# The 64-row tail of a gradient product on TensorE: full-height matmuls with zero rows, or pairs of half-height matmuls in runs across two steps

## The chip, the core and the metric

The kernel runs on one core of a Trainium2 chip. The metric is the device time of one execution in microseconds (us); lower is better. The engines are named as the profile names them: PE (TensorE, matmuls), PEld (its weight loads), DVE (VectorE), ACT (ScalarE), POOL (GpSimd) and SP (SyncE, which here only issues DMAs). Each engine runs its own instructions in a fixed order that is set when the program is built; they wait for one another through semaphores.

## The reference

The kernel computes a forward pass and all its gradients: a layer norm, a long convolution whose kernel comes from a state space model, and a gated feed-forward block (SwiGLU) that gates the convolution's result.

```python
def _B_ref(x, w1, w3, w2):
    gate = jnp.einsum("bsd,df->bsf", x, w1)
    up = jnp.einsum("bsd,df->bsf", x, w3)
    h = _silu(gate) * up
    out = jnp.einsum("bsf,fd->bsd", h, w2)
    return out

x = A_u                                   # 1 x 2048 x 576, bf16
xn = _layernorm(x, axis=-1)
s = _A_ref(xn, ...)                       # the convolution, by FFT
g = _silu(_B_ref(xn, B_w1, B_w3, B_w2))   # w1, w3: 576 x 4608, w2: 4608 x 576
out = x + s * g
# and the gradients of out for grad_out with respect to all inputs but B_x
```

The product around which the change stands is the gradient with respect to `h`. With `go` the gradient at the output of the feed-forward block (2048 tokens x 576), it is `gh = go @ w2.T` (2048 x 4608). It is summed over the 576 model columns. 576 is four times 128 and a rest of 64.

## The kernel before, in words

**Stages.** The kernel makes the forward feed-forward gate beside the forward convolution (0 to about 500 us of the profiled execution), then the feed-forward output and `go` (to about 640 us), then a backward stage of 18 *groups*, each of 256 of the 4608 hidden columns (`phase6_group`, from about 625 to 1321 us), and last the input gradients (`phase6_inputs`, to the end).

**One group of the backward stage** has on PE: (1) the product `gh` in four *steps* of `make(s)` (line L1936); (2) two pieces of the gradient of `w2` (`phase6_grad2`, L1977), one placed behind step 1 and one behind step 3; (3) the gradients of `w1` and `w3` (`phase6_grad13`, L2005, and for the last 64 model rows L2014 and L2016), which need the results of DVE on `gh`. In groups 0 to about 10 the backward convolution is fed in between (its transforms on PE at L932, L942 and L952, and long products on DVE at L963 to L971 and L1453); in groups 11 to 17 it is the sums for the state space parameters (PE at L1537, DVE at L1542 and L1545).

**The product `gh`.** A step makes 4 tiles of 128 tokens, k = 0, 1 in each half j = 0, 1 of the sequence, 256 hidden columns wide. Two PSUM banks (`ph[0]`, `ph[1]`, 128 x 512 in fp32) hold j = 0 and j = 1, with k = 0 and 1 side by side. Each tile is the sum of five matmuls, four over 128 model rows and a fifth, the *tail*, over the last 64. The tail also runs at 128 rows: the transposed `go` of the rest (`goTt`) has its lower 64 partitions set to zero by a memset (in `ffn_output`), and the columns of the row buffers of `w2` behind column 576 (`w2rows`, `backward`) are set to zero by a memset before the DMA transposes make `w2T` of them. So a step has 20 matmuls, a group 80, the kernel 1440, 288 of them tails:

```python
for k in range(2):
    t = s * 2 + k
    for j in range(2):
        ...
        steps.append((self.goTt[:, tt * P:(tt + 1) * P], w2T[:, :, nfull, :]))
```

ACT then copies the two banks to `gh` in bf16 (L1939), and DVE multiplies `gh` into two tiles `gu_n` and `gg_n` (L1954), which `phase6_grad13` reads and which SP stores.

**PSUM.** The eight banks of the backward stage are three for the product (`ps_h`), two for the weight gradients (`ps_gw`, tiles `pgw`, taken in turn by all of `phase6_grad2` and `phase6_grad13`) and three for the convolution and the parameter sums. A tile of a pool takes the bank used longest ago, and its first matmul waits until ACT has copied what stood there.

**Transposes of `go`.** `turn_go` turns each of the 16 tiles of `go` by five PE transposes to a PSUM tile and two ACT copies, the second for the rest of 64 rows (L1310 to L1312).

**The loads of `w2`.** `w2row_load` issues two DMAs per group from SP (L1830), 128 rows of 576 columns each; two groups later a pair of DMA transposes (L1851) makes `w2T`.

**What sets the order.** Every piece of work carries a due time (`self.at`), and a scheduler fixes each engine's order when the program is built, by due times, by the readiness it computes, and by `issue_after`, which puts one instruction behind another on the same engine. `self.sc` and `self.sp` keep ACT's copies and SP's DMAs in the order of the code.

The forward gate has a product of the same kind: at L1132 the 64-row rest of `w1` and of `w3` stand on partitions 0 to 63 and 64 to 127 and are multiplied as two matmuls of 64 rows and 512 columns, `pg` and `pu`, behind one another in the order. In the backward stage L2014 and L2016 are two matmuls of 64 output columns each, `gg_n` and `gu_n`, in turn.

## Time and profile before

| | us |
|---|---|
| median of the three timed runs | 1637.4 |
| the three runs | 1630.57, 1641.31, 1637.4 |
| the profiled execution's own time | 1642.12 |
| span from its first to its last instruction | 1640.3 |

| engine | busy us | share |
|---|---|---|
| PE | 1565.6 | 95% |
| DVE | 1386.0 | 84% |
| ACT | 840.3 | 51% |
| POOL | 516.9 | 32% |

A group of instructions is written with its line, engine, operation and tiles (out<-in), and its count; busy time counts time that two of its instructions share once, so that 1440 matmuls that each last 274 ns from start to end take 169.7 us, since the next begins while the last is still draining. The *pitch* below is the time from the start of one matmul to the start of the next. Where a row of the timeline merges several instructions, its time runs from the first one's start to the last one's end. In such rows 128*128 or 64*128 is the part of the array that a matmul uses, rows by columns of the weights.

### The profile page before, as it was taken

The numbers are of one execution on the slowest core, as the hardware profiler recorded it, in microseconds if no ns is written. First come the engines' busy times: TensorE is split into PE (matmuls) and PEld (weight loads), VectorE is DVE, ScalarE is ACT, GpSimd is POOL, SyncE is SP. The second block draws the span as 40 slices with busy tenths as digits, with TensorE's granted clock in tenths as the row PEclk, the third lists the DMA queues.
The fourth block names the chain that finished last, engine by engine and source line by source line (L and its number), as shares of the span: only waits on it lengthen the run. The fifth ranks groups of instructions, "written<-read, shape, count | busy, mean of one in ns | idle before, by whom it ended". The sixth has DMA issues, their size and how long they took to land. (4 is left out here: it accounts for less than half of the span.)

```text
span 1640.3 us, 34408 instructions
## 1 busy us (share of the span) xinstructions
PE 1565.6 (95%) x13331; PEld 1146.1 (70%) x13331; DVE 1386.0 (84%) x2145; ACT 840.3 (51%) x1520; POOL 516.9 (32%) x862
## 2 busy tenths in 40 slices
PE   6899999999999998999999999999999999998997
PEld 2454444444457777888888888888888787886786
DVE  8889999799965655998988999699999944987897
ACT  6989998766652115556555665655555401010011
POOL 6746765532252110111111111112212341524232
PEclk9999999999999999999999999999999999999999
DMA  7999999998999997576695756799999999999993
GB/s 237 344 346 362 373 347 382 371 271 250 324 284 217 236 208 229 158 216 195 190 252 164 213 186 183 207 262 243 266 259 250 245 245 245 240 195 201 241 230 87
DMA packets 616156, 408.26 MB, mean 249 GB/s; under 512 B 424698, under 2 KB 558426, under 8 KB 611386
## 3 DMA queue, kind: packets, MB, share of 16 engines
q1 hardware_dynamic: 561232, 277.45, 68.0%
q0 software_dynamic: 36576, 116.69, 21.7%
q10 hardware_dynamic: 18186, 11.95, 2.5%
q8 instruction: 104, 1.70, 0.4%
q14 instruction: 58, 0.48, 0.1%
HBM read 128.52 MB, written 188.76 MB: 193 GB/s over the span
## 5 line engine op out<-in xcount | busy, mean ns | idle before, releaser
L2005 PEld LDWEIGHTS <-xn_bf 128*128 128x128 bf16 x2304 | 224.2, 98 | 26.8 <-issue 0.8
L2059 PEld LDWEIGHTS <-acts 128*128 128x128 bf16 x1974 | 192.0, 98 | 56.8 <-DMA acts<-GG_dram 4.7
L1989 POOL DMA_DIRECT2D out_dram<-gw x72 | 47.2, 656 | 527.3 <-ACT gw L1983 285.1
L1542 DVE TENSOR_TENSOR pr_q<-et_ps,pz 128x1024 f32<-128x1024 f32 x144 | 176.0, 1222 | 34.7 <-PE et_ps L1537 25.5
L1123 PEld LDWEIGHTS <-xnT 128*128 128x128 bf16 x1152 | 107.7, 98 | 128.6 <-issue 21.1
L1545 DVE TENSOR_REDUCE S_all<-pr_q 128x32 f32<-128x1024 f32 x144 | 175.3, 1217 | 3.3
L1936 PE MATMUL ph<-w2T,goT 128*128 128x256 bf16 x1440 | 169.7, 274 | 1.4 <-ACT gh L1939 1.4
L1123 PE MATMUL pg<-wmB_w,xnT 128*128 128x512 bf16 x576 | 155.9, 379 | 2.3 <-DVE g_t L1142 1.8
L1936 PEld LDWEIGHTS <-goT 128*128 128x128 bf16 x1440 | 139.8, 98 | 19.2 <-issue 2.9
L1977 PE MATMUL pgw<-go_o,h_n 128*128 128x288 bf16 x1152 | 150.8, 287 | 1.0 <-ACT gw L1983 1.0
L1123 PE MATMUL pu<-wmB_w,xnT 128*128 128x512 bf16 x576 | 149.7, 379 | 0.0
L2059 PE MATMUL px<-wT,acts 128*128 128x288 bf16 x1134 | 145.8, 286 | 0.0
L2005 PE MATMUL pgw<-gu_n,xn_bf 128*128 128x256 bf16 x1152 | 132.1, 273 | 2.2 <-DVE gu_n L1954 2.1
L1977 PEld LDWEIGHTS <-h_n 128*128 128x128 bf16 x1152 | 112.3, 98 | 29.2 <-issue 2.1
L2005 PE MATMUL pgw<-gg_n,xn_bf 128*128 128x256 bf16 x1152 | 131.1, 273 | 0.0
L1939 ACT CAST gh<-ph 128x512 bf16<-128x512 f32 x144 | 80.5, 587 | 92.0 <-PE ph L1936 80.5
L1138 ACT ACTIVATE s_t<-pg 128x512 bf16<-128x512 f32 x144 | 88.5, 614 | 55.4 <-PE pu L1132 45.0
L2182 ACT ACTIVATE go<-gx 128x576 bf16<-128x576 f32 x15 | 10.3, 683 | 200.5 <-DVE gx L2130 195.1
L2059 PE MATMUL px<-wA,acts 128*128 128x288 bf16 x728 | 97.0, 289 | 7.8 <-DMA acts<-GU_dram 4.0
L813 POOL COPY KT<-k_s 64x128 bf16<-64x128 bf16 x144 | 84.5, 587 | 53.7 <-ACT k_s L810 49.0
L1143 ACT CAST u_t<-pu 128x512 bf16<-128x512 f32 x144 | 87.5, 608 | 6.3 <-PE pu L1123 6.2
L1152 POOL DMA_DIRECT2D G_dram<-g_t x72 | 51.5, 715 | 118.5 <-ACT g_t L1140 92.5
(338 smaller groups left out, 3244.3 us busy)
## 6 DMA issues: line engine op xcount, KB each, us to landing
U_dram<-u_t POOLq DMA_DIRECT2D x72, 256.0 KB, 6.0
H_dram<-h_t SPq DMA_DIRECT2D x72, 256.0 KB
G_dram<-g_t POOLq DMA_DIRECT2D x72, 256.0 KB, 5.8
Q_dram<-q_k SPq DMA_DIRECT2D x36, 512.0 KB
GG_dram<-gg_n SPq DMA_DIRECT2D x36, 512.0 KB
GU_dram<-gu_n SPq DMA_DIRECT2D x36, 512.0 KB
gg_n<-G_dram POOLq DMA_DIRECT2D x14, 1024.0 KB, 6.0
E_dram<-E_k SPq DMA_DIRECT2D x54, 256.0 KB
```

The lines of the kernel that those rows point to most:

```text
L813: nc.gpsimd.tensor_copy(out=KT[64 * hf:64 * hf + 64, :, ch // 9, h, d1:d1 + 8], in_=ks[64 * h:64 * h + 64, :, h, hf].rearrange("p d a -> p ...
L1123: ins = nc.tensor.matmul(pt[:], lhsT=xnT[:, c, ts], rhs=wm[w][:, c, :], start=(q == 0 and c == 0), stop=(q == 1 and c == nfull - 1))
L1138: nc.scalar.activation(out=s_t[:, :, q, :], in_=pgv, func=ACT.Silu)
L1143: self.gate_last = nc.scalar.copy(out=u_t[:, :, q, :], in_=puv)
L1152: self.u_stores[step] = nc.gpsimd.dma_start(out=dst[fb * ng:(fb + 1) * ng, :, i0:i0 + NT, :].rearrange("g p t f -> p g (t f)"), in_=src[:] ...
L1542: nc.vector.tensor_tensor(out=pr[:].rearrange("p r k e -> p r (k e)"), in0=T[x][:].rearrange("p z k h j a -> p (z k h j a)")[:, None].to_b ...
L1545: self.pr_last = nc.vector.tensor_reduce(out=self.S_all[:].rearrange("p r (h c) -> p r h c", h=2)[:, :, :, d0:d0 + 2], in_=pr[:].rearrange ...
L1936: self.pe_last = nc.tensor.matmul(ph[j][:, k, :].rearrange("p (a f) -> p a f", f=P), lhsT=lw, rhs=rh, start=(n == 0), stop=(n == nfull))
L1939: self.sc(lambda: nc.scalar.copy(out=gh[:, j], in_=ph[j][:]))
L1977: self.pe_last = nc.tensor.matmul(pgw[pi_][:, 0:pw], lhsT=hn[:, tt, fl * P:(fl + 1) * P], rhs=go_o[:, tt, po:po + pw], start=(tt == 0), st ...
L2005: self.pe_last = nc.tensor.matmul(pw_[:, 0:FG], lhsT=self.xn_bf[:, tt, c * P:(c + 1) * P], rhs=nat[:, tt, :], start=(tt == 0), stop=(tt == ...
L2059: self.pe_last = nc.tensor.matmul(px[pi_][:, 0:pw], lhsT=acts[i][:, ai, fi, :], rhs=w[:, po:po + pw], start=(n == 0), stop=(n == len(steps ...
```

## The change

1. The tail becomes a matmul of 64 rows. The turned rest of `go` for tokens of the first half (j = 0) stands on partitions 0 to 63 of `goTt`, that of the second half (j = 1) on partitions 64 to 127, and `w2T` holds the rest of `w2` on both halves of the partitions. The tails of j = 0 and j = 1 stand behind one another, as a pair that uses the upper and the lower half of the array.
2. The tails of two steps stand together. In 15 of the 18 groups a step pair (0, 1) or (2, 3) first has the full matmuls of k = 0 of both steps, then the eight tails (four pairs), then the full matmuls of k = 1. For that four banks are open at once: three of `ps_h` and, for j = 1 of the odd step, one tile of `ps_gw`. In groups 0, 2 and 8 (`LONE`) each step has its own run of four tails (two pairs), with two banks of `ps_h`, and nothing is taken of `ps_gw`.
3. The padding goes: the memsets on `goTt` and on `w2rows` fall away, and `w2row_load` issues a second DMA per 128 rows that puts columns 512 to 575 of `w2` once more behind column 576, so four DMAs per group in place of two.
4. `turn_go` makes the rest with a plain matmul against the identity to an fp32 area of a one-bank PSUM tile, on the partitions where the half belongs, in place of the fifth transpose; the ACT copy then reads fp32.

The number of matmuls stays the same. In the built order the 288 tails stand in 47 uninterrupted stretches: 27 of four pairs, 2 of three, 12 of two and 6 of one. The stretches that are cut up are those into which the scheduler put matmuls of the convolution: in groups 3, 5, 8 and 10. In groups 11 to 17 all 14 are whole. Two more things move. In groups 4 and 9 the last matmuls of `gh` stood 12 matmuls of L1977 ahead of `phase6_grad13`, and now stand 47 ahead of it. On DVE and ACT the order of some convolution products and copies against the ones on `gh` changes in groups 0 to 10. In groups 11 to 17 ACT's order is the same but for the bank that one copy in four reads, and on DVE the products of a pair's first step move behind a piece of the parameter sums. POOL's order is the same without the memsets; SP has two more issues of `w2row_load` in each group, each directly behind the one of the same rows.

PE, group 12, steps 2 and 3, before: the end of one accumulation and the start of the next. `ph_15894` and `ph_15895` are the banks of j = 0 and j = 1 of step 2.

```order
L1936 MATMUL ph_15894<-w2T_8884,goT_6965 128x256
L1936 LDWEIGHTS goT_6965
L1936 MATMUL ph_15895<-w2T_8884,goT_6965 128x256
L1936 LDWEIGHTS goT_6965
L1936 MATMUL ph_15895<-w2T_8884,goT_6965 128x256
```

The same place in the changed kernel: the last full matmul of k = 0 (`pgw_15932` is j = 1 of step 3, the bank from the weight gradients' pool), then the tails of step 2 (`ph_15921`, `ph_15922`) and of step 3 (`ph_15931`, `pgw_15932`) for k = 0, then the first tail for k = 1.

```order
L1935 MATMUL pgw_15932<-w2T_8883,goT_6965 128x256
L1935 LDWEIGHTS goT_6965
L1935 MATMUL ph_15921<-w2T_8883,goT_6965 128x256
L1935 LDWEIGHTS goT_6965
L1935 MATMUL ph_15922<-w2T_8883,goT_6965 128x256
L1935 LDWEIGHTS goT_6965
L1935 MATMUL ph_15931<-w2T_8883,goT_6965 128x256
L1935 LDWEIGHTS goT_6965
L1935 MATMUL pgw_15932<-w2T_8883,goT_6965 128x256
L1935 LDWEIGHTS goT_6965
L1935 MATMUL ph_15921<-w2T_8883,goT_6965 128x256
```

A tail stood last in each accumulation of five; now eight tails of four banks follow one another.

ACT, from the end of group 11 into group 12, before: the copies `gh` of steps 0 and 1, then those of the `w2` gradient.

```order
L2007 CAST gw_15616<-pgw 128x256
L2019 CAST gw13t<-pgw 128x256
L1939 CAST gh_15779<-ph 128x512 x2
L1939 CAST gh_15806<-ph 128x512 x2
L1983 CAST gw_15867<-pgw 128x288 x2
```

The same place in the changed kernel:

```order
L2036 CAST gw_15643<-pgw 128x256
L2048 CAST gw13t<-pgw 128x256
L1968 CAST gh_15806<-ph 128x512 x2
L1968 CAST gh_15847<-ph 128x512
L1968 CAST gh_15847<-pgw 128x512
L2012 CAST gw_15894<-pgw 128x288 x2
```

The order is the same; the fourth copy reads a `pgw` bank, and the second piece of the `w2` gradient, which takes that bank next, waits for it.

DVE, group 16, steps 2 and 3, before: the products of `gh` (of steps 2 and 3, `gh_17878` and `gh_17905`) among the parameter sums (`pr_q`, `S_all`).

```order
L1542 TENSOR_TENSOR pr_q<-et_ps,pz 128x1024
L1545 TENSOR_REDUCE S_all<-pr_q 128x16x2
L1542 TENSOR_TENSOR pr_q<-et_ps,pz 128x1024
L1954 TENSOR_TENSOR gu_n<-gh_17878,gu_n 128x2x512
L1545 TENSOR_REDUCE S_all<-pr_q 128x16x2
L1954 TENSOR_TENSOR gg_n<-gh_17878,gg_n 128x2x512
L1954 TENSOR_TENSOR gu_n<-gh_17905,gu_n 128x2x512
L1954 TENSOR_TENSOR gg_n<-gh_17905,gg_n 128x2x512
```

The same place in the changed kernel:

```order
L1547 TENSOR_TENSOR pr_q<-et_ps,pz 128x1024
L1550 TENSOR_REDUCE S_all<-pr_q 128x16x2
L1547 TENSOR_TENSOR pr_q<-et_ps,pz 128x1024
L1550 TENSOR_REDUCE S_all<-pr_q 128x16x2
L1983 TENSOR_TENSOR gu_n<-gh_17911,gu_n 128x2x512
L1983 TENSOR_TENSOR gg_n<-gh_17911,gg_n 128x2x512
L1983 TENSOR_TENSOR gu_n<-gh_17952,gu_n 128x2x512
L1983 TENSOR_TENSOR gg_n<-gh_17952,gg_n 128x2x512
```

The first product of the pair, `gu_n` of step 2, moved behind one reduction; the same instructions stand ahead of `gu_n` of step 3 as before.

The diff:

```diff
+    LONE = (0, 2, 8)
...
-            nc.gpsimd.memset(goTt[rem:P, :], 0.0)
...
     def turn_go(self, i, ptr, after=None):
         nc, cfg = self.nc, self.cfg
         nfull, rem = cfg.D // P, cfg.D % P
-        for c, (do, dsz) in enumerate(cfg.dch):
-            with self.tc.issue_after(after.ins) if after is not None else nullcontext():
-                nc.tensor.transpose(ptr[0:dsz, c, :], self.go_o[:, i, do:do + dsz], self.ident_bf[:])
-        nc.scalar.copy(out=self.goT[:, :, i * P:(i + 1) * P], in_=ptr[:, 0:nfull, :])
-        nc.scalar.copy(out=self.goTt[0:rem, i * P:(i + 1) * P], in_=ptr[0:rem, nfull, :])
+        half, t = divmod(i, cfg.LT // 2)
+        r = slice(rem * half, rem * half + rem)
+        full = ptr[:].bitcast(BF16)[:, 0:nfull * P].rearrange("p (c t) -> p c t", t=P)
+        tail = ptr[r, 256:256 + P]
+        with self.tc.issue_after(after.ins) if after is not None else nullcontext():
+            for c in range(nfull):
+                nc.tensor.transpose(full[:, c, :], self.go_o[:, i, c * P:(c + 1) * P], self.ident_bf[:])
+            nc.tensor.matmul(tail, lhsT=self.go_o[:, i, nfull * P:cfg.D], rhs=self.ident_bf[:], start=True, stop=True)
+        nc.scalar.copy(out=self.goT[:, :, i * P:(i + 1) * P], in_=full)
+        nc.scalar.copy(out=self.goTt[r, t * P:(t + 1) * P], in_=tail)
...
-            for w2r in self.w2rows:
-                nc.gpsimd.memset(w2r[:, :, D:cfg.DT * P], 0.0)
...
-            self.sp(lambda: self.nc.sync.dma_start(out=self.w2rows[gi % 2][:, fl, 0:D],
-                                                   in_=self.aps["B_w2"][fi * P:(fi + 1) * P, :]))
+            for o, d in ((0, 0), (D, D - D % P)):
+                self.sp(lambda: self.nc.sync.dma_start(out=self.w2rows[gi % 2][:, fl, o:o + D - d],
+                                                       in_=self.aps["B_w2"][fi * P:(fi + 1) * P, d:D]))
...
+        pairs = gi not in self.LONE
+        rem = D % P
+
+        def banks(s):
+            pools = (ps_h, "ph"), (ps_gw, "pgw") if pairs and s % 2 else (ps_h, "ph")
+            phs[s] = [pool.tile([P, 512], FP32, name=name)[:].rearrange("p (k f) -> p k f", k=2) for pool, name in pools]
+
+        def put(s, j, k, lhsT, rhs, start, stop, after):
+            with self.tc.issue_after(after.ins) if after is not None else nullcontext():
+                self.pe_last = nc.tensor.matmul(phs[s][j][:, k, :].rearrange("p (a f) -> p a f", f=P), lhsT=lhsT, rhs=rhs,
+                                                start=start, stop=stop)
+
+        def fulls(s, k, after):
+            for j in range(2):
+                tt = j * LH + s * 2 + k
+                for c in range(nfull):
+                    put(s, j, k, self.goT[:, c, tt * P:(tt + 1) * P], w2T[:, :, c, :], k == 0 and c == 0,
+                        k == 1 and c == nfull - 1, after if c == 0 else None)
+                after = self.pe_last
+
+        def tails(s, k):
+            t = s * 2 + k
+            for j in range(2):
+                r = slice(rem * j, rem * j + rem)
+                put(s, j, k, self.goTt[r, t * P:(t + 1) * P], w2T[r, :, nfull, :], k == 1, k == 0, self.pe_last)
 
         def make(s):
...
-            ph = [ps_h.tile([P, 2, FG], FP32, name="ph") for _ in range(2)]
+            run = (s, s + 1) if pairs and s % 2 == 0 else () if pairs else (s,)
+            after = None
+            for r in run:
+                banks(r)
+                fulls(r, 0, after)
+                after = self.pe_last
             for k in range(2):
-                t = s * 2 + k
-                for j in range(2):
-                    tt = j * LH + t
-                    steps = [(self.goT[:, c, tt * P:(tt + 1) * P], w2T[:, :, c, :]) for c in range(nfull)]
-                    steps.append((self.goTt[:, tt * P:(tt + 1) * P], w2T[:, :, nfull, :]))
-                    for n, (lw, rh) in enumerate(steps):
-                        self.pe_last = nc.tensor.matmul(ph[j][:, k, :].rearrange("p (a f) -> p a f", f=P), lhsT=lw, rhs=rh,
-                                                        start=(n == 0), stop=(n == nfull))
+                for r in run:
+                    tails(r, k)
+            fulls(s, 1, self.pe_last)
             for j in range(2):
-                self.sc(lambda: nc.scalar.copy(out=gh[:, j], in_=ph[j][:]))
+                self.sc(lambda: nc.scalar.copy(out=gh[:, j], in_=phs[s][j]))
             made[s] = gh
```

6 lines of the change are left out of this document (3 added, 3 removed).

## The prediction

> **What bounds the kernel now.** I read the first part of the page, then the busy time of the engines in the backward stage, window by window, then who waited for whom there. The page gives the span and the engines' shares:
>
> ```profile
> span 1640.3 us, 34408 instructions
> PE 1565.6 (95%) x13331; PEld 1146.1 (70%) x13331; DVE 1386.0 (84%) x2145; ACT 840.3 (51%) x1520; POOL 516.9 (32%) x862
> ```
>
> The share of 95% says that PE paces most of the time, not that it paces the stage that changes. The windows view gives, for windows of about a group each, the length, then the busy time of PE, PEld, DVE, ACT and POOL with their counts, the granted clock and DMA:
>
> ```profile
> 797.00:834.00 37.00, 35.75 (x349) 30.82 (x346) 36.28 (x66) 21.10 (x37) 4.76 (x8) 1.00 0.62 177
> 834.00:872.00 38.00, 37.01 (x374) 32.18 (x368) 25.30 (x47) 21.88 (x38) 4.78 (x8) 1.00 0.84 242
> 919.00:953.00 34.00, 32.65 (x323) 28.34 (x323) 34.00 (x64) 20.08 (x33) 4.92 (x9) 1.00 0.90 251
> ...
> 1177.00:1212.00 35.00, 35.00 (x352) 30.50 (x346) 33.48 (x37) 19.50 (x31) 7.23 (x13) 1.00 1.04 280
> 1212.00:1247.00 35.00, 35.00 (x350) 30.64 (x349) 33.47 (x37) 19.58 (x32) 8.23 (x15) 1.00 1.06 264
> 1247.00:1282.00 35.00, 35.00 (x353) 30.67 (x350) 33.47 (x38) 19.77 (x32) 7.71 (x14) 1.00 0.92 226
> ```
>
> Two regimes. In groups 14 to 16 (the last three windows) PE is busy for every microsecond and DVE has 1.5 us left in 35: PE paces, and DVE follows closely. In the groups with the convolution DVE is busy for 36.28 of 37 us and for 34.00 of 34, and PE has a microsecond or more of idle time; in the group at 834 DVE has 12.7 us to spare. There PE and DVE pace each other in turn. The waits between 681 and 1071 us show both directions, PE's first, then DVE's:
>
> ```profile
> PE et_ps L952 <- DVE Z L970: 4.1, 6, 1.0
> PE et_ps L942 <- DVE ZZ L1453: 4.1, 7, 1.0
> PE pgw L2005 <- DVE gu_n L1954: 2.1, 2, 1.4
> PE et_ps L942 <- DVE gk_st L1473: 1.9, 1, 1.9
> PE pgw L1977 <- ACT gw L1983: 1.0, 2, 0.5
> ```
>
> ```profile
> DVE gg_n L1900 <- ACT gg_n L1907: 22.6, 3, 11.2
> DVE gx L1501 <- PE et_ps L952: 5.3, 5, 1.8
> DVE Z L963 <- ACT g L934: 4.1, 3, 2.4
> ```
>
> **What a tail costs today.** The changed matmuls are one group of rows, and one group of 15 shows how they run:
>
> ```profile
> L1936 PE MATMUL ph<-w2T,goT 128*128 128x256 bf16 x1440 | 169.7, 274 | 1.4 <-ACT gh L1939 1.4
> ```
>
> ```profile
> 1221.22 4.53 PE L1936 MATMUL ph<-w2T,goT 128*128 128x256 bf16 x40
> 1225.59 4.08 PE L1977 MATMUL pgw<-go_o,h_n 128*128 128x288 bf16 x32
> 1229.51 0.61 PE L1537 MATMUL et_ps<-gz,qT 128*128 128x128 bf16 x8
> 1229.96 5.40 PE L2005 MATMUL pgw<-gu_n,xn_bf 128*128 128x256 bf16 x48
> ```
>
> Forty matmuls from first start to last end take 4.53 us, and a single one 0.27, so the pitch is (4.53 - 0.27) / 39 = 0.109 us. A tail of 64 useful rows costs the same 0.109 as a full matmul; eight cost 0.873, and 288 cost 31.4.
>
> **What a pair costs.** No matmul of 64 rows by 256 columns is in the trace. Two neighbours are. The forward gate's tails are pairs of 64 rows, with 512 columns:
>
> ```profile
> 252.09 0.81 PE L1123 MATMUL pu<-wmB_w,xnT 128*128 128x512 bf16 x3
> 252.84 0.39 PE L1132 MATMUL pg<-wtail,xnT 64*128 64x512 bf16 x1
> 252.84 0.39 PE L1132 MATMUL pu<-wtail,xnT 64*128 64x512 bf16 x1
> 253.06 0.38 PE L1132 MATMUL pg<-wtail,xnT 64*128 64x512 bf16 x1
> 253.06 0.38 PE L1132 MATMUL pu<-wtail,xnT 64*128 64x512 bf16 x1
> 253.37 0.60 PE L1123 MATMUL pg<-wmB_w,xnT 128*128 128x512 bf16 x2
> ```
>
> The two of a pair start together. The full pitch is (0.81 - 0.38) / 2 = 0.215, so the last full matmul starts at 252.52. The first pair starts 0.31 later instead of 0.215, the second pair 0.22 after the first, the next full matmul 0.31 after that. Going into the half-height form and coming out of it each cost about 0.095 us beyond a pitch. The other neighbour has this width of 256 columns, but splits the array by columns:
>
> ```profile
> 950.65 0.60 PE L2005 MATMUL pgw<-gg_n,xn_bf 128*128 128x256 bf16 x4
> 951.18 0.30 PE L2014 MATMUL pgw<-gg_n,xn_bf 128*64 128x256 bf16 x1
> 951.19 0.30 PE L2016 MATMUL pgw<-gu_n,xn_bf 128*64 128x256 bf16 x1
> 951.32 0.27 PE L2014 MATMUL pgw<-gg_n,xn_bf 128*64 128x256 bf16 x1
> ...
> 952.85 0.27 PE L2014 MATMUL pgw<-gg_n,xn_bf 128*64 128x256 bf16 x1
> ...
> 953.05 0.50 PE L1936 MATMUL ph<-w2T,goT 128*128 128x256 bf16 x3
> ```
>
> The last full matmul starts at 950.65 + 3 x 0.11 = 950.98; in: 0.20; first to second pair 0.13 to 0.14; then 14 pitches to the sixteenth pair in 1.53, 0.109 each; out: 0.20. For the new runs I take in 0.205 and out 0.202 (0.109 plus the row pairs' 0.096 and 0.093), the first pair's pitch 0.133 and each further one 0.109, as the neighbour of the same width shows. From the last full matmul to the next:
>
> - four pairs: 0.205 + 0.133 + 2 x 0.109 + 0.202 = 0.758 in place of 9 x 0.109 = 0.981: 0.223 saved
> - three pairs 0.114 saved, two pairs 0.005, one pair 0.080 lost.
>
> With 27, 2, 12 and 6 stretches that is 6.02 + 0.23 + 0.06 - 0.48 = 5.8 us of PE time. If every pair had the dear pitch of 0.133 it would be 4.5; if every one had 0.109, 6.8. 3.1 us of the 5.8 lie in the 14 runs of groups 11 to 17, 2.7 in groups 0 to 10, where the cut-up runs are.
>
> The Trainium skill ("TensorEngine Tiling (Array Packing)", Overview) gives up to two times the speed for a contraction of at most 64; by that alone the tails would cost half of 31.4, a gain of 15.7 us. The same page (Tiling Modes) says that a change of mode drains the engine; the 0.31 where 0.215 was due agrees, and the rows above, which hold that price, decide for 5.8.
>
> **What of it reaches the end.** In groups 11 to 17 a group gets 2 x 0.223 = 0.45 us shorter on PE. DVE has 1.5 us left per group, so it can follow. The close place is `gu_n`, which L2005 reads:
>
> ```profile
> 1228.26 0.69 DVE L1954 TENSOR_TENSOR gu_n<-gh,gu_n 128x1024 bf16<-128x1024 bf16 x1
> ...
> 1229.94 1.23 DVE L1542 TENSOR_TENSOR pr_q<-et_ps,pz 128x1024 f32<-128x1024 f32 x1 [0.39 <-PE et_ps L1537]
> ```
>
> It is done at 1228.95, and L2005 starts at 1229.96: 1.0 us to spare. DVE has the same instructions ahead of it after the change, and falls back into step with PE in every group (the wait of 0.39). So PE's 0.45 leaves 0.5 to spare, and all 3.1 us count.
>
> In groups 0 to 10 what PE saves ahead of a wait on DVE is given back in a longer wait, unless DVE itself waited for PE. PE waits there 10.1 us for `Z`, `ZZ` and `gk_st`; DVE waits 9.4 for what PE feeds (`gx`, and `Z` by way of ACT). That is about even, so I take half of 2.7, 1.4 us, with 0 and 2.7 as ends. The reordering of DVE and ACT there has no price in the trace; by the nearest waits I allow -2 to +2 us around 0. To the good side speaks that the wait of 2.1 us for `gu_n` falls where 47 matmuls now stand in place of 12 (5.7 us in place of 1.5).
>
> **Edits costed at nothing.** The memsets were on POOL, busy 32%. The plain matmul in `turn_go` has the same operands and size as the transpose it replaces; the copy that reads fp32 is at most some 0.1 us longer sixteen times on ACT, which is half idle. The 36 more DMA issues take SP:
>
> ```profile
> L1830 SPq DMA_DIRECT2D w2r<-in_B_w_dram x36: 328/432/2065, 524.9 to 1196.8; - x36
> ```
>
> 0.43 us each, 0.9 per group, ahead of loads queued on SP behind them; SP itself waits in every group for PE to free buffers, and the rows are needed a group later. Without that cover each group could lose up to 0.9 us, 16 in all; I see nothing that takes the cover away.
>
> Sum: 3.1 + 1.4 = 4.5 us. The profiled execution took 1642.1, 4.7 above the median, so it becomes 1637.6, and against the median of 1637.4 the forecast is 1632.9.
>
> **Rivals.**
>
> *The fourth bank comes late (slower).* Behind step 3 the first piece of the `w2` gradient takes 16 x 0.122 = 1.95 us; the second piece then needs the bank that ACT's fourth copy empties. The copies and ACT's other work:
>
> ```profile
> L1939 ACT CAST gh<-ph 128x512 bf16<-128x512 f32 x144 | 80.5, 587 | 92.0 <-PE ph L1936 80.5 <-DVE gg_n L1954 5.7 <-DVE h_n L1901 5.3
> 1228.17 1.28 ACT L1904 ACT_TABLE_LOAD   x1
> 1229.46 1.06 ACT L1904 ACTIVATE gu_n<-gg_n 128x1024 bf16<-128x1024 bf16 x1
> ```
>
> Four copies take 4 x 0.587 = 2.35 us and can begin 12 matmuls (1.31 us) ahead of the last matmul's start, plus 0.27 for a matmul to end: done 1.3 us behind it, 0.65 before the bank is needed. If ACT came to them late by a table load and an activation (2.34 us), PE would stand 1.7 us in each of 30 runs, 51 us, less 4.5: 1683.5. It decides from a lateness of 0.65 us. Against it: ACT waited for PE before these copies, 80.5 us in all. The Trainium skill ("TensorEngine Tiling (Array Packing)", Performance Considerations) warns that tiling speeds up the matmuls but not the evacuation of PSUM; no row here shows it as the limit yet.
>
> *The pairs do not overlap.* Each matmul of 64 rows then takes its own 0.109, and each of 47 stretches loses its way in and out, 0.19 us: 8.9 us, 1646.3. Against it: two starts at 252.84.
>
> *No drain between the forms.* The page's factor two then holds: 3.1 becomes 56 pairs x 0.109 = 6.1, the rest half of 88 x 0.109, 4.8: 10.9 us, 1626.5, with everything on the path 1621.7. The 0.31 speaks against it.
>
> *DVE paces everything.* Then all is given back, 1637.4. The 35.00 of 35 against 33.47 speak against it.
>
> **How the numbers follow.** The forecast 0.70; DVE paces 0.13; pairs one by one 0.06; the late bank 0.05; no drain 0.04; a reordering worse than allowed 0.02. The likeliest case's own range: a gain of 14 x 0.175 = 2.4 (dear pitch, nothing from groups 0 to 10) to 6.8 + 2 = 8.8, so 1628.6 to 1635.0. The three runs before spread by 10.7 us, so a median of a few moves by some 3 either way; with that and "DVE paces" the range is 1625 to 1642. One per cent, 16.4 us, is about what a measurement of this kernel can tell from no change. Faster by that would need all of the drain-free case and a fast set of runs: 0.03. Slower by that needs the late bank or a bad reordering: 0.05. Within: 0.92.
>
> **What would show it.** Pairs of L1935 (the new line of the product) that start within 0.01 us; 0.20 in and out and 0.11 to 0.13 between pairs; windows of groups 14 to 16 shorter by 0.45, with PE still busy throughout; no wait of PE for `gh` copies by L2006 (the `w2` gradient). Wrong would be: a wait of PE for `gu_n` in groups 11 to 17, a wait of L2006 for ACT in most groups, or a pair pitch near 0.22.

## The result, and the profile after

The changed kernel took 1650.85 us (median of six executions) beside 1631.2 us for the kernel before, also of six: a ratio of 1.0113, with a 95% interval of 1.0082 to 1.0143. A ratio here leaves out executions more than 1.5% above the fastest of their kernel, a median does not, so the two need not agree. Two further sets gave 1.0115 (1.0065 to 1.0164) and 1.0084 (1.0044 to 1.0125). The forecast was 1632.9, a small gain, in a range of 1625 to 1642. The kernel became slower by 14 to 19 us.

The first trace of the changed kernel is of its longest execution (1671.8 us). So the trace of its third set, whose span lies nearer to the median, is read below. Its page begins:

```profile
span 1648.8 us, 34434 instructions
PE 1561.8 (95%) x13331; PEld 1127.3 (68%) x13331; DVE 1387.7 (84%) x2145; ACT 837.4 (51%) x1520; POOL 514.8 (31%) x859
```

PE is busy for 3.8 us less than before (1565.6), and the span is 8.5 us longer, so PE waits longer. The windows view says where. I cut the program at the first and the last matmul of the product with `hc` (the forward hidden values, by which the output is made), and behind groups 0, 10 and 17. Columns: window, length, busy time of PE, PEld, DVE, ACT and POOL with counts, granted clock, DMA share, GB/s. First the kernel before:

```profile
476.80:637.40 160.60, 159.66 (x1291) 122.90 (x1290) 89.63 (x127) 36.30 (x69) 31.61 (x56) 1.00 0.97 223
637.40:681.10 43.70, 39.30 (x373) 33.22 (x371) 36.51 (x67) 30.91 (x57) 4.25 (x7) 0.96 0.69 218
681.10:1071.00 389.90, 376.33 (x3736) 326.50 (x3735) 350.78 (x630) 228.88 (x410) 50.01 (x84) 1.00 0.69 199
1071.00:1321.40 250.40, 245.73 (x2423) 213.73 (x2423) 237.99 (x261) 128.63 (x211) 55.79 (x98) 1.00 1.05 251
1321.40:1640.30 318.90, 302.62 (x2601) 242.88 (x2599) 237.29 (x333) 32.24 (x65) 111.17 (x202) 0.98 1.08 210
```

Then the changed kernel:

```profile
473.90:649.30 175.40, 161.57 (x1291) 123.24 (x1290) 89.89 (x127) 37.33 (x70) 30.20 (x54) 0.96 1.00 205
649.30:693.30 44.00, 38.84 (x366) 31.16 (x364) 36.46 (x66) 31.05 (x56) 4.25 (x7) 0.96 0.69 217
693.30:1089.70 396.40, 376.81 (x3743) 316.97 (x3742) 352.22 (x631) 227.57 (x410) 50.01 (x84) 0.99 0.69 197
1089.70:1342.20 252.50, 243.91 (x2424) 206.74 (x2423) 239.00 (x261) 126.11 (x211) 55.74 (x98) 0.99 1.08 251
1342.20:1648.80 306.60, 300.02 (x2601) 242.58 (x2601) 237.13 (x333) 32.23 (x65) 111.55 (x202) 0.99 1.08 217
```

The stage of `hc` is 14.8 us longer, groups 1 to 10 6.5, groups 11 to 17 2.1. The last stage is 12.3 shorter, and that is not the change: over all traces of this study it takes 307 to 326 us, and one and the same kernel (the two runs of the version with late runs below) took 325.0 and 307.6. PE's busy time, too, is 2.6 us shorter in this last stage, and only 1.8 in groups 11 to 17. A single trace of this kernel carries some 10 us of such chance, so its stages are compared here and the totals only over many executions.

**The pairs do what was forecast.** The timeline of PE in group 12 of the changed kernel; a row is a series with its start, the time to its last end, its operands and its count:

```profile
1128.31 0.60 PE L1935 MATMUL pgw<-w2T,goT 128*128 128x256 bf16 x4
1128.84 0.39 PE L1935 MATMUL ph<-w2T,goT 64*128 64x256 bf16 x3
1128.96 0.27 PE L1935 MATMUL pgw<-w2T,goT 64*128 64x256 bf16 x1
1129.07 0.38 PE L1935 MATMUL ph<-w2T,goT 64*128 64x256 bf16 x3
1129.18 0.27 PE L1935 MATMUL pgw<-w2T,goT 64*128 64x256 bf16 x1
1129.38 1.49 PE L1935 MATMUL ph<-w2T,goT 128*128 128x256 bf16 x12
```

The last full matmul starts at 1128.31 + 0.60 - 0.27 = 1128.64. The first pair is 0.20 behind it, the fourth pair 0.34 behind the first (three pitches of 0.113), the next full matmul 0.20 behind that: 0.74 in place of 0.981 for nine full pitches. Two such stretches save 0.48 per group; the groups without a wait show 0.44, since they now take 34.31 us in place of 34.75 with PE busy throughout:

```profile
1126.60:1160.90 34.30, 34.30 (x347) 29.31 (x346) 33.32 (x37) 19.13 (x31) 7.87 (x14) 1.00 1.07 236
1267.70:1302.00 34.30, 34.30 (x345) 29.33 (x346) 33.31 (x37) 19.13 (x31) 7.32 (x13) 1.00 1.05 262
```

**Where the time went.** PE's waits in two windows of the changed kernel, the first from 600 to 720 us, the second around group 6; neither has its like at these places in the trace of before (the dots part the two views):

```profile
PE po L1249 <- DMA hcA<-H_dram: 11.8, 1, 11.8
...
PE pgw L2034 <- DVE gu_n L1983: 4.4, 1, 4.4
```

The first wait is for a load that the change does not touch, the last transposed load of `hcA`. SP's own timeline shows what stands ahead of it (start, time, operation, count; SPq means issuing):

```profile
599.98 8.28 SPq L1855 DMA_TRANSPOSE hcC<-H_dram  x1
608.30 0.57 SPq L1834 DMA_DIRECT2D w2r<-in_B_w_dram  x1
608.98 0.41 SPq L1271 DMA_DIRECT2D GS_dram<-gs_t  x1
609.43 2.13 SPq L1834 DMA_DIRECT2D w2r<-in_B_w_dram  x2
611.66 0.38 SPq L1279 DMA_DIRECT2D odd_out<-o  x1
612.13 15.60 SPq L1855 DMA_TRANSPOSE hcA<-H_dram  x1
```

Three loads of `w2` rows, two of them small, now lie between `hcC` and `hcA`. POOL meanwhile issues two loads of 1 MB for group 0, `gg_n` and `h_n`. First POOL in the changed kernel, then SP and POOL before:

```profile
613.59 0.53 POOL L1859 DMA_DIRECT2D gg_n<-G_dram  x1 [0.42 <-issue]
624.21 0.53 POOL L1859 DMA_DIRECT2D h_n<-U_dram  x1 [10.09 <-PE po L1249]
```

```profile
611.54 6.84 SPq L1851 DMA_TRANSPOSE hcA<-H_dram  x1
```

```profile
617.63 0.53 POOL L1855 DMA_DIRECT2D gg_n<-G_dram  x1
```

Before, SP had all but finished issuing `hcA` (618.38) when the first 1 MB load came; after, they run together, and issuing `hcA` takes 15.60 us in place of 6.84. By the clock `hcA` starts only 0.6 us later and `gg_n` 4.0 us earlier; but the stage of `hc` began 2.9 us earlier here, so counted from its start `hcA` is 3.5 us late and `gg_n` 1.1 us early. What the DMA engines moved meanwhile stands in the last columns of two windows, first after, then before:

```profile
630.00:635.00 5.00, 0.00 (x0) 0.00 (x0) 0.00 (x0) 0.00 (x0) 0.00 (x0) 0.50 1.02 91
```

```profile
620.00:625.00 5.00, 5.00 (x44) 3.92 (x42) 2.91 (x5) 1.05 (x3) 0.00 (x0) 1.00 0.98 336
```

At the same busy share (1.02 and 0.98) they moved 91 GB/s in place of 336. The two windows do not hold the same loads: in the second, SP is done with issuing `hcA` and most of what moves is `gg_n`; in the first, `gg_n` has landed (14.0 us after its issue, in place of 7.6 before), and what is left of `hcA` moves beside `h_n`. What `hcA` moves alone stands below, with the run that holds the large loads back: 187 GB/s. Of the 7829 packets between 608 and 632 us 7294 are under 512 bytes, and 155 have 8 KB or more. The Trainium skill ("DMA: Bandwidth & Descriptors", Queues, rings and completion order) says that each DMA engine takes turns between queues packet by packet. That would make the small packets of a transposed load wait behind the large ones of `gg_n` and `h_n`; the drop agrees, and no run here looks at the turns themselves.

The second wait is in group 6, and is there in every trace with runs across two steps in that group. ACT's copies and DVE's products there, first before, then after:

```profile
878.49 1.13 ACT L1939 CAST gh<-ph 128x512 bf16<-128x512 f32 x2 [1.20 <-PE ph L1936]
```

```profile
873.81 0.76 DVE L963 TENSOR_TENSOR Z<-g,a 128x1152 bf16<-128x1152 bf16 x1 [2.37 <-ACT g L934]
...
880.16 0.69 DVE L1954 TENSOR_TENSOR gu_n<-gh,gu_n 128x1024 bf16<-128x1024 bf16 x1
...
900.27 0.69 DVE L1954 TENSOR_TENSOR gu_n<-gh,gu_n 128x1024 bf16<-128x1024 bf16 x1
```

```profile
891.58 1.56 ACT L1968 CAST gh<-ph 128x512 bf16<-128x512 f32 x3 [2.40 <-PE ph L1935]
```

```profile
885.71 0.76 DVE L964 TENSOR_TENSOR Z<-g,a 128x1152 bf16<-128x1152 bf16 x1 [2.37 <-ACT g L935]
...
896.19 0.69 DVE L1983 TENSOR_TENSOR gu_n<-gh,gu_n 128x1024 bf16<-128x1024 bf16 x1
...
915.04 0.69 DVE L1983 TENSOR_TENSOR gu_n<-gh,gu_n 128x1024 bf16<-128x1024 bf16 x1
```

Counted from the group's first `Z`, the first copies come 5.9 us in (4.7 before), since the first full matmuls of both steps and all their tails stand ahead of them. The first `gu_n` comes 10.5 us in (6.35 before), behind one more piece of the convolution, and the last 29.3 (26.5 before). DVE has hardly a gap there, so the place in its order decides; the weight gradient reads `gu_n`, and PE stands for 4.4 us. The window from 884.0 to 935.5 us, group 6, has a granted clock of 0.93, where the group had 1.00 before: the group is 5.1 us longer, a little more than the wait.

### The profile page after: what moved, and what is told of

It reads as the page before. It is cut to its first block, busy times and chain, and to the rows that moved or that the text cites. A ratio compares the mean times of both kernels' runs of the same rounds, so it can differ in the third digit from the quotient of the medians.

```text
span 1669.8 us, 34434 instructions
## 1 busy us (share of the span) xinstructions
PE 1565.7 (94%) x13331; PEld 1130.1 (68%) x13331; DVE 1388.1 (83%) x2145; ACT 837.2 (50%) x1520; POOL 515.5 (31%) x859
## 2 busy tenths in 40 slices
DMA packets 621341, 408.86 MB, mean 245 GB/s; under 512 B 429882, under 2 KB 563610, under 8 KB 616570
## 5 line engine op out<-in xcount | busy, mean ns | idle before, releaser
L1935 PEld LDWEIGHTS <-goT 128*128 128x128 bf16 (+1 forms) x1440 | 120.4, 98 | 34.1 <-issue 19.1
L1935 PE MATMUL ph<-w2T,goT 128*128 128x256 bf16 (+1 forms) x1140 | 139.0, 276 | 0.6 <-ACT gh L1968 0.6
L1968 ACT CAST gh<-ph 128x512 bf16<-128x512 f32 x114 | 60.2, 593 | 98.8 <-PE ph L1935 92.8
L1153 POOL DMA_DIRECT2D G_dram<-g_t x72 | 51.5, 715 | 122.9 <-ACT g_t L1141 99.3
```

Source lines behind the costliest of these rows:

```text
L1153: self.u_stores[step] = nc.gpsimd.dma_start(out=dst[fb * ng:(fb + 1) * ng, :, i0:i0 + NT, :].rearrange("g p t f -> p g (t f)"), in_=src[:] ...
L1935: self.pe_last = nc.tensor.matmul(phs[s][j][:, k, :].rearrange("p (a f) -> p a f", f=P), lhsT=lhsT, rhs=rhs, start=start, stop=stop)
L1968: self.sc(lambda: nc.scalar.copy(out=gh[:, j], in_=phs[s][j]))
```

## The experiments

Each was timed beside runs of the kernel before on its chip, with twelve executions (six for the first repeat of the changed kernel and the first run with the gate). A ratio is to the kernel before, with its 95% interval.

### The changed kernel again

No edit.

> The changed kernel once more, for a second trace. Its first trace shows the steady groups 12 and 15 at 34.31 us in place of 34.75, as forecast, and yet 24 us more up to the end of group 0, where PE stood 23.3 us for a late transposed load of the forward hidden values (hcA), and 10 us of waits for the loads of qT. Theory A, the small loads: the 36 added loads of 128 x 64 disturb the queue and its neighbours, so the waits for hcA and qT come back here in the same places, with 10 us or more together, and the time is 1.0 to 1.3% above the kernel before. Theory B, a passing disturbance of that one execution: no wait for a load over 3 us, and a trace within 5 us of the kernel before; the 1.1% would then have to sit elsewhere (the groups 0 to 10, PE against DVE).

> The changed kernel again, on the chip of the three above. 1.007 to 1.014 of before; in its trace group 6 at 50 to 51 us, the groups without waits for loads at 34.31, and the stage of the forward hidden values above 165 us if hcA is still being issued when gg_n is, at 160 if not.

Measured: 1.0115 (1.0065 to 1.0164) and 1.0084 (1.0044 to 1.0125). In both traces the stage of `hc` is long (185.5 and 175.4 us against 160.6 before), group 6 takes 51.3 and 51.5 us against 46.45, and the groups without a wait 34.31. Theory B, a passing disturbance, falls; that the small loads are the cause, as theory A has it, is not yet shown.

### The small loads alone, and the change without them

The small loads in the kernel before (the padded weights stay zero, so the product is as before):

```diff
-            for w2r in self.w2rows:
-                nc.gpsimd.memset(w2r[:, :, D:cfg.DT * P], 0.0)
...
-            self.sp(lambda: self.nc.sync.dma_start(out=self.w2rows[gi % 2][:, fl, 0:D],
-                                                   in_=self.aps["B_w2"][fi * P:(fi + 1) * P, :]))
+            for o, d in ((0, 0), (D, D - D % P)):
+                self.sp(lambda: self.nc.sync.dma_start(out=self.w2rows[gi % 2][:, fl, o:o + D - d],
+                                                       in_=self.aps["B_w2"][fi * P:(fi + 1) * P, d:D]))
```

> The kernel before with only the small loads: the padding of the w2 rows is filled by the 36 loads of 128 x 64 in place of the two memsets; the weights of the padded rows stay zero, so the product is as before, with full-height tails. Theory A (the small loads cost the time): 10 to 17 us slower than before, ratio 1.006 to 1.010, with waits of PE for hcA or qT. Theory B: within 3 us of before (ratio 0.998 to 1.002).

Measured: 1.0076 (1.0034 to 1.0118), 12.4 us, with nothing else of the change in it; in its trace PE waits for `hcA` and the stage of `hc` takes 169.6 us.

The changed kernel without them (it leaves the tail of the second half of the tokens out of the gradient of `h`):

```diff
+            for w2r in self.w2rows: nc.gpsimd.memset(w2r[:, :, D:cfg.DT * P], 0.0)
...
-            for o, d in ((0, 0), (D, D - D % P)):
+            for o, d in ((0, 0),):
```

> The changed kernel without the small loads: the rows 64 to 127 of the tail of w2 stay zero (memset as before), so the tail of the second half of the tokens is left out of the gradient of h; every matmul and its order stay. Theory A: 3 to 5 us faster than before (ratio 0.997 to 0.998), the gain that the pairs were forecast to bring. Theory B (the time is lost in the order of PE, DVE and ACT, not in the loads): 10 to 17 us slower than before, as the changed kernel.

Measured: 1.0036 (1.0009 to 1.0064), between the two theories: the loads are most of the loss, but the rest of the change, forecast to gain 4.5 us, loses 5.9 (1.5 to 10.5). Its trace has group 6 at 50.4 us, with PE's wait of 4.4 us for `gu_n`.

### Runs within a step in all groups

```diff
-    LONE = (0, 2, 8)
+    LONE = tuple(range(18))
```

> The changed kernel with the runs kept within one step in all 18 groups: 72 runs of two pairs, no fourth bank from the pool of the weight gradients, steps in the order of before; the small loads stay. By the prices of the prediction two pairs save 0.005 us a run, so PE is as before. Theory A: as the changed kernel within 4 us (10 to 17 us slower than before). Theory C (the fourth bank or the two-step order costs the time): within 3 us of before.

Measured: 1.0053 (1.0017 to 1.009), between the two again: with the small loads in it, it is 8.7 us slower than before, but groups 1 to 10 take 389.3 us, as before (389.9), with group 6 at 46.44. The long group 6 belongs to the runs across two steps. Its groups without waits take 34.72 to 34.73 us (34.75 before): pairs in runs of two gain next to nothing, as priced.

### What it is about the small loads

Issued by ACT in place of SP:

```diff
-                self.sp(lambda: self.nc.sync.dma_start(out=self.w2rows[gi % 2][:, fl, o:o + D - d],
-                                                       in_=self.aps["B_w2"][fi * P:(fi + 1) * P, d:D]))
+                put, q = (self.sc, self.nc.scalar) if o else (self.sp, self.nc.sync)
+                put(lambda: q.dma_start(out=self.w2rows[gi % 2][:, fl, o:o + D - d], in_=self.aps["B_w2"][fi * P:(fi + 1) * P, d:D]))
```

> The changed kernel with its 36 small loads issued by ACT in place of SP (a few rows of PE, DVE and ACT change places with it in groups 0 to 10). So far the small loads alone made the kernel before about 12 to 22 us slower, and without them the changed kernel is 12 us nearer to before. Theory Q (their place in SP's queue, where they hold back the transposed loads behind them): the cost goes; 1.003 to 1.005 of before, as the changed kernel without them. Theory P (their packets of 128 bytes themselves, on whichever queue): as the changed kernel, 1.008 to 1.014.

Measured: 1.0025 (0.9991 to 1.006), no more than the change without small loads. The same packets on another queue cost nothing that this can see, which speaks for theory Q; a few us more or less would not show. Its trace, of an execution of 1665.08 us, has the meeting of `hcA` and `gg_n` all the same (the stage of `hc` takes 179.6 us).

Left out for groups 0 and 1 (the gradient of `h` lacks the tail of the second half of the tokens there):

```diff
-            for o, d in ((0, 0), (D, D - D % P)):
+            for o, d in ((0, 0), (D, D - D % P))[:1 + (gi > 1)]:
```

> The changed kernel with the small loads of groups 0 and 1 left out (the tail of the second half of the tokens is missing from the gradient of h in these two groups), those of groups 2 to 17 kept. Theory S (the start: the small loads hold the transposed load of hcA back until it meets the 1 MB load of gg_n; PE stood 23.3 and 14.3 us there in the two traces of the changed kernel): as without any small loads, 1.003 to 1.005 of before. Theory L (they disturb loads anywhere): 1.007 to 1.013.

Measured: 1.0089 (1.0052 to 1.0126), the figure of theory L, but the edit does not part the two theories. In its trace SP issues the rows of groups 0 and 1 at 522 and 545 us; those directly ahead of `hcA` (614.23) belong to groups 2 and 3, and their four small loads are still there, two ahead of `hcC` and two behind it. PE waits 9.5 us for `hcA`, and the stage takes 174.7 us. So the loads at the start were not taken away, and theory S is not tested.

Then, in the kernel before, its own loads cut in two, so that SP issues 36 more loads of no more bytes, in pieces of 576 or of 1024 and 128 bytes a row:

```diff
+            for o, e in ((0, 288), (288, D)):
-            self.sp(lambda: self.nc.sync.dma_start(out=self.w2rows[gi % 2][:, fl, 0:D],
-                                                   in_=self.aps["B_w2"][fi * P:(fi + 1) * P, :]))
+                self.sp(lambda: self.nc.sync.dma_start(out=self.w2rows[gi % 2][:, fl, o:e],
+                                                       in_=self.aps["B_w2"][fi * P:(fi + 1) * P, o:e]))
```

> The kernel before with each load of w2 rows cut into two halves of 288 columns: 36 more loads on SP, as many as the small loads, but packets of 576 bytes and no more bytes than before; all else as before. The small loads on SP cost the kernel before 12 to 22 us, and nearly nothing on ACT. Theory N (the number of loads on SP counts): 1.006 to 1.012 of before. Theory P2 (the packets of 128 bytes count, on SP's queue): within 0.998 to 1.003.

> The kernel before with each load of w2 rows cut at column 512: again 36 more loads on SP and the bytes of before, but the second piece has 64 columns, packets of 128 bytes. Theory N: as the even cut, 1.006 to 1.012. Theory P2: 1.006 to 1.012 here, and the even cut within 0.998 to 1.003. If neither cut costs anything, what the small loads cost lies in the bytes added or in the second read of the same columns.

Measured: 1.0040 (1.0005 to 1.0076) for the even cut and 1.0064 (1.0027 to 1.0101) for the cut at 512. The even cut lies below theory N's figure and above theory P2's, the other within N's. Both cost, and their intervals overlap: packets of 128 bytes are not needed for a cost. The Trainium skill ("DMA: Bandwidth & Descriptors", Specifications) puts the least transfer for full rate at 512 bytes; the pieces of the even cut lie above it, so that rule does not explain their cost. More loads also make more packets, 621341 in the trace of the even cut against 616156 before. The run with both copies in one load, below, has 620764, with no load more, and costs no more than the change without small loads (616156). That speaks for the number of loads that SP issues.

One small load for both halves of a group in the kernel before, 18 in place of 36:

```diff
+        f0 = gi * nfl * P
+        self.sp(lambda: self.nc.sync.dma_start(out=self.w2rows[gi % 2][:, :, D:self.cfg.DT * P],
+            in_=self.aps["B_w2"][f0:f0 + nfl * P, D - D % P:D].rearrange("(n p) d -> p n d", p=P)))
```

> The kernel before with one small load per group, both halves in one (18 in place of 36, the same 4608 packets of 128 bytes); no memset of the padding. Theory N: half of the cost of the 36, 1.004 to 1.006. Theory P2: the whole, 1.007 to 1.013.

Measured: 1.0044 (1.0004 to 1.0083), within theory N's figure, and not clear of theory P2's. It has nearly as many packets as the 36 small loads (621052 and 621341), so this too points to the loads; but the intervals of all four kernels with added loads overlap.

### Both copies of the tail in one load

In the changed kernel columns 256 to 319 of D become the tail. One load of two overlapping pieces of 320 columns then brings the tail twice, side by side, and nothing is added to SP's queue:

```diff
-            for o, d in ((0, 0), (D, D - D % P)):
...
+            src = self.aps["B_w2"][fi * P:(fi + 1) * P, :]
+            self.sp(lambda: self.nc.sync.dma_start(out=self.w2rows[gi % 2][:, fl].rearrange("p (a q) -> p a q", a=2),
+                                                   in_=bass.AP(src.tensor, src.offset, [[D, P], [256, 2], [1, 320]])))
...
-                nc.tensor.transpose(full[:, c, :], self.go_o[:, i, c * P:(c + 1) * P], self.ident_bf[:])
+                nc.tensor.transpose(full[:, c, :], self.go_o[:, i, (0, 128, 320, 448)[c]:][:, 0:P], self.ident_bf[:])
...
-                put(s, j, k, self.goTt[r, t * P:(t + 1) * P], w2T[r, :, nfull, :], k == 1, k == 0, self.pe_last)
+                put(s, j, k, self.goTt[r, t * P:(t + 1) * P], w2T[r, :, 2, :], k == 1, k == 0, self.pe_last)
```

> The changed kernel without added loads and with the full result: the tail is made from columns 256 to 319 of D in place of the last 64, so that one load of two overlapping pieces of 320 columns brings both copies (packets of 640 bytes in place of 1152 and 128); PE, ACT, DVE and POOL keep their order. If the small loads are the cause, by either theory: 1.002 to 1.005 of before, with group 6 still 4 to 5 us longer than before (50 to 51 us against 46.45) and groups 12 to 16 at 34.31. If a second piece per row is enough to disturb: 1.008 to 1.014.

Measured: 1.0027 (0.9994 to 1.0059), as without small loads. Groups 1 to 10 take 394.1 us in its trace.

The same with runs across two steps only in groups 11 to 17:

```diff
-    LONE = (0, 2, 8)
+    LONE = tuple(range(11))
```

> The same with the runs across two steps only in groups 11 to 17; groups 0 to 10 keep the order of before with pairs within a step. If the small loads and the order in group 6 are the two losses, both are gone: group 6 at 46.4 us, groups 12 to 16 at 34.31, 3 to 4 us faster than before (ratio 0.9975 to 0.998). If something else in the change costs time: 1.000 or more.

> The kernel with one overlapping load and the runs across two steps in groups 11 to 17 alone, once more, for its interval: its trace shows groups 11 to 16 at 34.31 us and no group longer than before. Theory: the forecast gain of 3 to 4 us is there (0.9975 to 0.998 over both sets of runs together). Rival: the gain on PE is lost in the last stage, in waits for the acts loads (13.6 us there in its first trace, 6 us or less in others): 1.000 to 1.003.

Measured: 1.0028 (0.9996 to 1.006) and 0.9975 (0.9937 to 1.0013), the first outside the expected figure, the second in it. In the traces both losses are gone. Group 6 and group 12 of the first:

```profile
865.10:911.50 46.40, 44.08 (x443) 36.30 (x442) 44.56 (x80) 26.68 (x52) 4.14 (x8) 1.00 0.53 167
1097.90:1132.20 34.30, 34.30 (x346) 29.32 (x346) 33.31 (x37) 19.14 (x31) 7.91 (x14) 1.00 1.12 266
```

From the end of group 0 to that of group 17 it takes 634.8 and 633.5 us against 640.3 before. In a third trace of these groups, with the gate of the next section, it is 641.6, since PE waits 5.7 us for a load of `gz` in group 11. So the gain is in the steady groups, a single wait for a load is larger than it, and in the total it is not told from zero.

### Holding back the load of `gg_n`

Over the fourteen traces so far the stage of `hc` took 160.3 to 160.6 us where POOL issued `gg_n` when SP was done with `hcA` or within 0.8 us of it, and 167 to 186 us in the nine where SP was still at it for 3 to 18 us. With added loads ahead of `hcA` on SP (the run without those of groups 0 and 1 is one of these) seven of eight traces are among the nine, without them two of six: the meeting also comes by chance, and the loads seem to make it likelier. To make the meeting impossible, POOL copies one value of `hcA` first, which waits for that load to land:

```diff
+                if i == LT - 1:
+                    self.hc_gate = nc.gpsimd.tensor_copy(out=self.persist.tile([P, 2], BF16, name="hcg")[0:1, 0:1],
+                                                         in_=hc[FT - 1][0][0:1, FT - 1 - hc[FT - 1][1], 0:1])
...
+        with self.tc.issue_after(self.hc_gate.ins) if gi == 0 else nullcontext():
+            self.group_load(gi > self.SYNC, gg, self.G_dram[gi])
```

In the changed kernel, twice:

> The changed kernel, small loads and all, with one POOL instruction added: a copy of one value of hcA ahead of POOL's load of gg_n for group 0, so that this 1 MB load cannot be issued before hcA has landed. Theory M (the meeting of the two loads is what the small loads cost in this stage): the stage of the forward hidden values (first to last matmul of the product with hc) takes 160 to 163 us in place of 185, PE's wait for hcA is under 3 us, and the time comes down by 5 us or more, to 1.004 to 1.008 of before; what is left is the order in group 6 and the waits for qT. Rival (hcA is late by itself, since SP issues it late): the stage stays at 170 us or more, no gain.

> The changed kernel with the gate once more. If the meeting carries most of the cost of the small loads: 1.003 to 1.007 of before, below the 1.0084 to 1.0115 of the changed kernel. If the cost comes elsewhere, or the gate gives it back later: 1.008 or more.

SP's row for `hcA` in the first, then POOL's rows:

```profile
613.53 5.22 SPq L1858 DMA_TRANSPOSE hcA<-H_dram  x1
```

```profile
620.93 0.18 POOL L1242 COPY hcg<-hcA 1x1 bf16<-1x1 bf16 x1 [10.19 <-DMA hcA<-H_dram]
622.79 0.54 POOL L1862 DMA_DIRECT2D gg_n<-G_dram  x1
```

Issuing `hcA` takes 5.22 us, and PE no longer waits for it. The DMA engines meanwhile, with `hcA` nearly alone:

```profile
613.50:618.70 5.20, 5.20 (x45) 4.15 (x43) 3.16 (x5) 0.65 (x1) 0.00 (x0) 1.00 0.95 187
```

The stage takes 161.9 and 164.9 us (what is left in the second is a wait of 3.5 us for `e`), and 161.8 to 166.0 in all five traces with the gate. So the meeting is what made this stage long. The total: 1.0101 (1.0047 to 1.0154) and 1.0065 (1.0026 to 1.0103), one as without the gate and one below; the stage came out as theory M has it, the total of the first did not.

In the kernel before with the small loads alone, and in the kernel before itself:

> The kernel before with the 36 small loads on SP and the gate. Without the gate it stood at 1.0076 (1.0034 to 1.0118), the gate alone at 1.0021. If the meeting carries the cost: 1.001 to 1.004, the stage at 162 us. If not: 1.006 to 1.011 with the stage at 162 us.

> The kernel before with the same gate alone. Theory M: the kernel before meets the same collision in some of its executions; 0 to 3 us faster, 0.998 to 1.000. If the gate itself delays group 0: 1.001 to 1.003.

Measured: 1.0062 (1.0022 to 1.0103), with the stage at 166.0 us, and 1.0021 (0.9977 to 1.0064), which does not tell whether the gate itself costs. Against 1.0076 without the gate the gain is within the intervals. The medians of all twelve executions of the small loads, 1657.1 without and 1641.4 with the gate (the kernel before beside them: 1635.1 and 1637.4), would say that the meeting carries most of the cost; the ratios do not. How much of the 12 us it carries stays open.

On top of the version with both losses mended:

> The kernel with one overlapping load and two-step runs in groups 11 to 17 alone, plus the same gate. Theory M: that kernel met gg_n late in both of its traces (160.3 us in the stage), but some of its untraced executions will not have; the gate takes those away: 1 to 4 us below it, 0.994 to 0.998 of before. Rival: gg_n comes 2 to 4 us later and the first group waits for it: no gain, or up to 4 us more.

Measured: 0.998 (0.9943 to 1.0018). Over the 36 executions of that version, with and without the gate, the mean is 1633.9 us, beside 1635.9 over the 157 of the kernel before: 2 us better, with a standard error of 1.5. It is clearly better than the changed kernel and not shown to be better than the kernel before.

## Why the prediction was wrong

**The price of a pair: right.** 0.20 in, 0.113 a pair, 0.20 out against 0.205, 0.133 and 0.109, and 0.202; the whole stretch 0.74 against 0.758. The neighbours of equal width and of equal shape, put together, gave it. "The pairs do not overlap" and "no drain between the forms" are ruled out by the same rows.

**Groups 11 to 17: nearly right.** 0.44 a group against 0.45, but in six groups, not seven: group 17 stayed at 39.8 us (39.75 before). That makes 2.6 of the forecast 3.1. In group 17 DVE is busy for 38.8 of 39.8 us before the change, so DVE paces it, and what PE saved went into waits; "all 3.1 us count" was read from groups 14 to 16 alone.

**The late fourth bank: did not come.** No wait of the `w2` gradient for `gh` copies stands in any trace. (By its own terms, 1637.4 + 51 - 4.5, this rival's time is 1683.9 and not 1683.5.) "DVE paces everything" did not come in groups 11 to 16 either: where no wait for a load falls in them, PE is busy for 34.30 of 34.30 us.

**"Edits costed at nothing": the step that failed most.** The 36 loads on SP were bounded by 16 us from above, from 0.43 us each, and then dropped: "I see nothing that takes the cover away". Alone they cost 12.4 us (5.5 to 19). The cover that I named, SP's waits for buffers and the rows' own late due time, says nothing of the transposed loads of `hcC` and `hcA` behind them, and PE then stood for `hcA` (11.8 us in the trace above). SP's timeline of before already showed `hcA` and `gg_n` passing each other with 0.75 us of overlap. So the bound was of the right size, and by the prediction's own rule it belonged in the range, with a chance of its own; the range would then have reached to about 1649 (1637.4 + 16 - 4.5), still short of the measured 1650.85; the next step failed as well.

**Groups 0 to 10: the sign was wrong.** 1.4 us of gain were forecast, with -2 to +2 for the order. The trace of the changed kernel has +6.5 for groups 1 to 10. Over all traces the nine with runs across two steps in these groups take 394.1 to 396.6 us there, the eleven others, pairs within a step among them, 387.4 to 389.9: runs across two steps cost some 7 us there in the mean, about 4 to 5 of them in group 6. The step failed because it priced PE's matmuls and gave DVE's order a symmetric allowance. But a run across two steps makes the first copies of a pair later, since PE work of the second step moved ahead of them (5.9 us in place of 4.7 in group 6), and in most of these groups DVE has 0 to 3 us of slack. I also took the 47 matmuls ahead of the wait for `gu_n` as cover for it, in groups 4 and 9; group 6 got the wait.

**Together.** The 12.4 us of the loads alone and the 5.9 that the rest loses without them make 18.3, within the measured 14 to 19; both have wide intervals.

**What is left open.** How the 36 loads cost 12 us. The meeting in the stage of `hc` is one part; the gate takes it away, and its effect on the total lies within the intervals. In groups 11 to 17 of the changed kernel PE also waits for `qT` and `gz` (3.6 and 2.4 us in its third trace, 1.7 together before), but in the kernel before with the small loads it waits 1.3 us there, so that these waits come from the loads is not shown. No run takes away just the small loads ahead of `hcA`. So the place of most of the 12 us is not settled.

## What to carry to other kernels

A load that costs its queue half a microsecond is priced by what is queued behind it and by whom that then meets, not by when its own data is due; look for the next load on that queue that something waits for, and for the large load on another queue that it has to stay ahead of. When a change joins two steps to make runs longer, ask which engine gets its first input later, and use it only where that engine has slack. If a bound has been worked out, it belongs in the range unless a row of the trace shows the cover.

## What the runs showed of the hardware

A transposed load and 1 MB loads from two queues do far worse together than one after the other: issuing the first took 15.6 us in the trace shown, and 5.2 to 7.1 in the ten traces in which SP was done with it, but for 0.75 us at most, when the large load came. In five microseconds of the meeting the DMA engines moved 91 GB/s while busy at a share of 1.02; with the transposed load nearly alone it was 187 at 0.95, with mostly the large load 336 at 0.98.

The same 36 loads cost 12.4 us (5.5 to 19) on SP's queue, in the kernel before, and nothing measurable on ACT's, in the changed kernel (1.0025 against 1.0027 and 1.0036 without them).

And a stall of PE costs a little more than itself: in the window of the stall quoted above, in which PE did nothing, the granted clock is 0.50, and the 1291 matmuls of that stage kept PE busy for 161.57 us in place of 159.66.
